# A new order for the attention turn of an attention and soft mixture-of-experts kernel

## The chip, the cores and the metric

The kernel runs on one core of a Trainium2 chip. TensorE (PE) multiplies, VectorE (DVE) reduces and does elementwise work, ScalarE (ACT) copies and takes exponentials, GpSimd (POOL) copies, and SyncE (SP) issues nearly all DMAs. Each engine takes its instructions in program order and waits for others through semaphores. The metric is the device time of one execution in microseconds; the median of three runs is compared.

## What is computed

Block attention over q, k, v of shape (8, 8, 576, 64), in chunks of 64 positions, then a soft mixture of 8 experts over the 4608 rows of 512 numbers that the attention gives.

```
scores = scale * matmul(q_c, k_c^T)             # per (batch, head, chunk): 64 x 64
attn   = exp(scores - max); attn /= sum(attn) + 1e-9
x      = matmul(attn, v_c), heads side by side  # 4608 x 512
logits = x @ phi                                # 4608 x 32
d      = softmax of logits over the rows;    slot_input = d.T @ x
slot_out[e] = relu(slot_input[e] @ w1[e]) @ w2[e]        # 8 experts
c      = softmax of logits over the 32 slots;    out = c @ slot_out
```

All is float32.

## The kernel before

**Stages.** An attention stage of 36 turns, then an expert stage. A turn handles 512 positions of two heads (`unit(t)`: block `n = t // 4`, head pair `t % 4`). Four turns make one block, whose logits and running softmax sums follow in the turns after it. Blocks 0 to 3 come first, then the block made of the last 64 positions of all batches, then 4 to 7.

**One turn t**, by function. SP loads k, q (`load_qk`, 256 KB each) and v (`load_v`, 2 x 128 KB) into three buffers each. POOL reorders k and q by head (`pair_heads`, L166). PE turns each with four transposes (`turn_qk`, L170), ACT copies the turned tiles out of PSUM (`place_qk`, L175 to L191), PE multiplies the scores into `psc` (`scores`, L199), DVE takes the maximum and subtracts it (`s_sub`, L210 and L211), ACT exponentiates (`s_exp`, L217), PE transposes the result into bank 0 of `pav` (`turn_p`, L231), ACT copies it to `at` (`place_p`, L235), PE multiplies with v into all four banks of `pav` (`values`, L244), DVE sums the exponentials and takes reciprocals (`s_sum`, L221 to L224) and normalises `pav` into x (`norm_x`, L252). PE then transposes x (`turn_x`, L260) and ACT copies it to `xT` (`place_x`, L263).

**Once per block**, spread over four successive turns: logits of the block (`logits`, L270) with its running maximum (`maxima`) and exponentials (`weights`); their transposes (`natural`, L310) with `natural_copy` and `shifted` (L322, L324); the partial slot sums (`partial`, L354) and `partial_add` (L365) with `combination`; and `turn_c`, `place_c`.

**What sets the order.** The program text, engine by engine; nothing is reordered. In the loop (L425 to L486) `values` of turn t-1 stands at the end of iteration t and `norm_x` of it at the start of iteration t+1. PSUM has eight banks: `pav` four, `psc` two, `pg` and `ph` one each. Where one of the block steps holds `ph`, the turned q goes to bank 2 of `pav` (`pq = pav[:, 2]`), from iteration 6 on in every iteration.

**Weights.** Of 32 weight tiles of 1 MB (two DMAs of 512 KB each), 17 are loaded during the attention into the pool `wpa` (L426, L427). The next five go to the pool `wpb` (L516), whose memory is that of the attention's buffers, so each waits for the last reader of what lay there; the last ten go to `wpa` tiles as the first expert matmuls (`up`, L532) release them (`refill`). All of these issues stand in SP's one queue. The second expert matmuls are `down` (L566); `combine` and `store` make and write the output.

Of the kernel before, what the change touches and what calls it, by code (L numbers as in the profile page):

```python
# [15 lines left out]
def kernel(  # L16
# [29 lines left out]
    NWB = 5  # L46
    NQ, NV, NX = 3, 3, 7
# [59 lines left out]
    with ExitStack() as actx:  # L107
# [5 lines left out]
        qn = [st.tile([P, 2, 4, D], F32, name=f"qn{i}") for i in range(NQ)]  # L113
        kn = [st.tile([P, 2, 4, D], F32, name=f"kn{i}") for i in range(NQ)]
        vn = [st.tile([P, 2, 2, 2, D], F32, name=f"vn{i}") for i in range(NV)]
        qp = st.tile([P, 4, 2, D], F32, name="qp")
        kp = st.tile([P, 4, 2, D], F32, name="kp")
        qT = [st.tile([P, 8 * CH], F32, name=f"qT{i}") for i in range(2)]
        kT = [st.tile([P, 8 * CH], F32, name=f"kT{i}") for i in range(2)]
        sct = [st.tile([P, 2, 8, 32], F32, name=f"sc{i}") for i in range(2)]  # L120
        at = st.tile([P, 2, 2, P], F32, name="at")
        xr = [st.tile([P, 4, P], F32, name=f"x{i}") for i in range(NX)]
        xT = [st.tile([P, 4, P], F32, name=f"xT{i}") for i in range(NHP)]
# [42 lines left out]
        def pair_heads(t):  # L166
            nc.gpsimd.tensor_copy(kp.rearrange("p j a d -> p a j d"), kn[t % NQ])  # L167
            nc.gpsimd.tensor_copy(qp.rearrange("p j a d -> p a j d"), qn[t % NQ])  # L168
# [6 lines left out]
        def place_qk(t, isk, src):  # L175

            n, b, hp = unit(t)
            o = (kT if isk else qT)[t % 2]
            if isk and b < NB - 1:
                o = o.rearrange("x (c u p j) -> x j u c p", c=8, u=2, j=2)  # L180
                i = src.rearrange("x (j u c p) -> x j u c p", c=8, u=2, j=2)
            elif isk:
                o = o.rearrange("x (c u p j) -> x j u p c", c=8, u=2, j=2)
                i = src.rearrange("x (j u p c) -> x j u p c", c=8, u=2, j=2)
            elif b < NB - 1:
                o = o.rearrange("x (y j) -> x j y", j=4)
                i = src.rearrange("x (j y) -> x j y", j=4)
            else:
                o = o.rearrange("x (c p j) -> x j p c", c=8, j=4)
                i = src.rearrange("x (j p c) -> x j p c", c=8, j=4)  # L190
            nc.scalar.copy(o, i)  # L191
# [58 lines left out]

        def norm_x(t):
            nc.vector.tensor_tensor(  # L252
                xr[t % NX].rearrange("p l (a d) -> p l a d", d=D),
# [4 lines left out]
        def turn_x(t):  # L258
            for l in range(4):
                nc.tensor.transpose(out=pg[:, P * l:P * (l + 1)], in_=xr[t % NX][:, l], identity=ident)  # L260
# [4 lines left out]
        lst, cms, cns = {}, {}, {}  # L265
# [20 lines left out]
        def weights(n):  # L286
            pl = ph[:, 0:P]
            no, nn = nm_run[(n + 1) % 2], nm_run[n % 2]
            eT = sm.tile([P, P], F32, tag="eT", name=f"eT_{n}")
            es = sm.tile([P, 1], F32, tag="es", name=f"es_{n}", bufs=2)  # L290
            nc.scalar.activation(eT, pl, AF.Exp, bias=nn, accum_out=es)
            lT = sm.tile([P, P], F32, tag="lT", name=f"lT_{n}")
# [5 lines left out]
            lst[n] = (eT, lT, al, es)  # L298

        def sums(n):  # L300
            al, es = lst[n][2:]
# [6 lines left out]
        def natural(n):  # L308
            eT, lT = lst[n][:2]
# [3 lines left out]
        def natural_copy(n):  # L313
            eT, lT, al, es = lst[n]
            eN = sm.tile([P, 4, SL], F32, tag="eN", name=f"eN_{n}")
            nc.scalar.copy(eN.rearrange("p l s -> p (l s)"), ph[:, 0:P])
            lst[n] = (eN, lT, al, es)

        def shifted(n):
# [3 lines left out]
            cc = sm.tile([P, 4, SL], F32, tag="cc", name=f"cc_{n}")  # L323
            nc.vector.tensor_tensor(cc, lv, cm.to_broadcast([P, 4, SL]), ALU.subtract)  # L324
            cms[n] = cc

        def combination(n):


            cc = cms.pop(n)  # L330
            nc.scalar.activation(cc, cc, AF.Exp)
# [4 lines left out]
            cn = sm.tile([P, 2, 2, SL], F32, tag="cn", name=f"cn_{n}")  # L336
# [5 lines left out]
            cns[n] = cn  # L342

        def turn_c(n):
            nc.tensor.transpose(out=ph[:, 0:P], in_=cns.pop(n).rearrange("p M w s -> p (M w s)"), identity=ident)
# [4 lines left out]
        def partial(n, dst):  # L350
            eN = lst[n][0]
# [315 lines left out]
```

## Time and profile before

| | us |
|---|---|
| median of three runs (295.39 to 300.87) | 296.06 |
| the profiled execution | 296.35 |
| its span | 294.6 |
| PE busy | 220.6 |
| DVE busy | 146.7 |
| ACT busy | 144.5 |
| POOL busy | 67.0 |

The span is the time from the first to the last instruction of the profiled execution; 1.75 us of its time lie around it. Busy time adds up the instructions of an engine. Matmuls are pipelined, so PE's busy time overstates how much of it is used. The chain of waits names, from the end backwards, what released each instruction that mattered.

### The profile page before, as it was taken

How to read it: one execution, taken by the hardware profiler on the slowest of the kernel's cores; microseconds unless marked ns; L12 is line 12 of the kernel's file. 1: busy time of each engine (PE TensorE's matmuls, PEld its weight loads, DVE VectorE, ACT ScalarE, POOL GpSimd, SP SyncE). 2: the span in 40 equal slices, each digit the busy share in tenths (PEclk: the TensorE clock that was granted, in tenths of full speed). 3: DMA queues.
4: the chain of work that ended last, by engine and by line, in shares of the span. 5: the costliest groups of instructions: out<-in, count | busy, mean ns of one | idle time of the engine just before them, and what ended most of it. 6: DMA issues, size and time to landing. Idle time of an engine off the chain costs nothing.

```text
span 294.6 us, 11946 instructions
## 1 busy us (share of the span) xinstructions
PE 220.6 (75%) x5196; PEld 167.7 (57%) x5196; DVE 146.7 (50%) x339; ACT 144.5 (49%) x277; POOL 67.0 (23%) x149
## 2 busy tenths in 40 slices
PE   8797876877786886886786676796665999978800
PEld 8575765766665675675675665675543235535400
DVE  0386638746656666666756845855521000026800
ACT  1776465655756865764774675565311010025700
POOL 2531133114135852312312411310104000000000
PEclk9999999979999999999999999997955899999955
DMA  7988888667997789797886785642009999997997
GB/s 209 326 277 261 285 249 236 210 207 211 301 262 195 206 267 277 225 301 244 230 286 206 205 255 173 185 122 96 2 2 294 416 396 358 348 296 236 316 328 298
DMA packets 60292, 72.15 MB, mean 245 GB/s; under 512 B 4688, under 2 KB 50768, under 8 KB 60240
## 3 DMA queue, kind: packets, MB, share of 16 engines
q1 hardware_dynamic: 59728, 70.86, 77.0%
q8 instruction: 41, 0.67, 1.0%
q0 software_dynamic: 512, 0.53, 0.7%
q14 instruction: 11, 0.09, 0.1%
HBM read 61.93 MB, written 9.44 MB: 242 GB/s over the span
## 4 chain that ended last, share of the span: by engine, by line
PE 38%; ACT 22%; DVE 20%; issue 6%; DMA 5%; SPq 3%; POOL 1%; DVEq 0%; ACTq 0%; POOLq 0%
ACT qT L191 12%; PE pav L244 7%; PE ph L532 5%; DVE x L252 5%; PE pav L172 5%; PE pav L231 5%; ACT at L235 4%; DVE mx L210 4%; PE ph L270 3%; SPq L102 3%; DMA w<-in_moe_w_dram 3%; DVE sc L211 3%; PE pg L172 3%; DVE su L221 2%; PE ph L132 2%
## 5 line engine op out<-in xcount | busy, mean ns | idle before, releaser
L244 PE MATMUL pav<-vn,at 32*64 32x64 f32 x2304 | 37.9, 232 | 18.4 <-ACT at L235 16.0
L244 PEld LDWEIGHTS pav<-vn,at 32*64 32x64 f32 x2304 | 32.5, 134 | 23.7 <-ACT at L235 20.8
L217 ACT ACTIVATE sc<-sc 128x512 f32<-128x512 f32 x36 | 22.7, 630 | 45.6 <-DVE sc L211 45.6
L167 POOL COPY kp<-kn 128x512 f32<-128x512 f32 x36 | 22.1, 614 | 87.4 <-issue 55.5
L191 ACT COPY qT<-pav 128x512 f32<-128x512 f32 x29 | 31.8, 1097 | 14.8 <-PE pav L231 11.9
L210 DVE TENSOR_REDUCE mx<-psc 128x8 f32<-128x512 f32 x36 | 24.6, 683 | 27.4 <-PE psc L199 27.4
L191 ACT COPY kT<-pg 128x512 f32<-128x512 f32 x36 | 24.3, 675 | 19.0 <-PE pg L172 18.2
L172 PE MATMUL pav<-ident,qp 128*128 128x128 f32 x116 | 18.2, 280 | 19.0 <-DVE x L252 19.0
L199 PE MATMUL psc<-kT,qT 64*64 64x64 f32 x1152 | 26.4, 227 | 2.8 <-issue 2.8
L252 DVE TENSOR_TENSOR x<-pav,rc 128x512 f32<-128x512 f32 x36 | 24.7, 687 | 6.3 <-PE pav L244 6.3
L199 PEld LDWEIGHTS psc<-kT,qT 64*64 64x64 f32 x1152 | 21.0, 136 | 9.4 <-issue 9.4
L172 PEld LDWEIGHTS pav<-ident,qp 128*128 128x128 f32 x116 | 12.9, 143 | 23.2 <-POOL cn L341 9.7
L211 DVE TENSOR_TENSOR sc<-psc,mx 128x512 f32<-128x512 f32 x36 | 24.9, 692 | 1.2
L231 PE MATMUL pav<-ident,sc 128*128 128x128 f32 x144 | 22.3, 278 | 3.8 <-ACT sc L217 3.6
L168 POOL COPY qp<-qn 128x512 f32<-128x512 f32 x36 | 22.1, 614 | 12.6 <-PE pav L172 11.8
L221 DVE TENSOR_REDUCE su<-sc 128x8 f32<-128x512 f32 x36 | 24.4, 678 | 0.9 <-ACT sc L217 0.7
L172 PE MATMUL pg<-ident,kp 128*128 128x128 f32 x144 | 23.2, 284 | 0.9 <-issue 0.5
L235 ACT COPY at<-pav 128x512 f32<-128x512 f32 x36 | 22.8, 633 | 1.9 <-PE pav L231 1.9
L260 PE MATMUL pg<-ident,x 128*128 128x128 f32 x144 | 22.8, 282 | 1.0 <-DVE x L252 0.7
L263 ACT COPY xT<-pg 128x512 f32<-128x512 f32 x36 | 21.6, 600 | 2.4 <-PE pg L260 2.4
L231 PEld LDWEIGHTS pav<-ident,sc 128*128 128x128 f32 x144 | 16.9, 143 | 5.3 <-ACT sc L217 4.8
L172 PEld LDWEIGHTS pg<-ident,kp 128*128 128x128 f32 x144 | 16.3, 143 | 4.4 <-issue 3.2
(86 smaller groups left out, 286.8 us busy)
## 6 DMA issues: line engine op xcount, KB each, us to landing
w<-in_moe_w_dram SPq DMA_DIRECT2D x64, 512.0 KB, 5.9
kn<-in_k_dram SPq DMA_DIRECT2D x32, 256.0 KB, 4.8
qn<-in_q_dram SPq DMA_DIRECT2D x32, 256.0 KB, 5.0
vn<-in_v_dram SPq DMA_DIRECT2D x64, 128.0 KB, 3.7
out_dram<-ob SPq DMA_DIRECT2D x8, 512.0 KB, 4.1
out_dram<-ob SPq DMA_DIRECT2D x4, 1024.0 KB, 7.8
kn<-in_k_dram SPq DMA_DIRECT2D x8, 128.0 KB, 5.4
qn<-in_q_dram SPq DMA_DIRECT2D x8, 128.0 KB, 5.0
```

The lines of the kernel that those rows point to most:

```text
L172: nc.tensor.transpose(out=dst[:, P * j:P * (j + 1)], in_=(kp if isk else qp)[:, j].rearrange("p a d -> p (a d)"), identity=ident)
L191: nc.scalar.copy(o, i)
L199: nc.tensor.matmul(psc[CH * M:CH * (M + 1), a, P * l:P * l + CH], lhsT=qT[t % 2][r, c], rhs=kT[t % 2][r, c], start=True, stop=True,)
L210: nc.vector.reduce_max(mx, pv, axis=AX.X)
L211: nc.vector.tensor_tensor(sct[t % 2].rearrange("p u r i -> p r u i"), pv.rearrange("p r (u i) -> p r u i", u=2), mx.unsqueeze(2).unsqueeze ...
L217: nc.scalar.activation(sct[t % 2], sct[t % 2], AF.Exp, scale=SCALE)
L221: nc.vector.reduce_sum(su, sct[t % 2].rearrange("p u r i -> p r u i"), axis=AX.XY)
L231: nc.tensor.transpose(out=pav[:, 0, o:o + P], in_=sct[t % 2][:, u, 4 * a:4 * (a + 1)].rearrange("p l i -> p (l i)"), identity=ident)
L235: nc.scalar.copy(at.rearrange("p a u x -> p (a u x)"), pav[:, 0])
L244: nc.tensor.matmul(pav[CH * M:CH * (M + 1), l, D * a:D * (a + 1)], lhsT=at[r, a, u, CH * M:CH * (M + 1)], rhs=vv[r, M, a, u, :], start=(u ...
L252: nc.vector.tensor_tensor(xr[t % NX].rearrange("p l (a d) -> p l a d", d=D), pav[:, :, 0:P].rearrange("p l (a d) -> p l a d", d=D), rcs.po ...
L260: nc.tensor.transpose(out=pg[:, P * l:P * (l + 1)], in_=xr[t % NX][:, l], identity=ident)
```

## The change

The loop body is written anew. `scores` and `s_sub` of turn t now stand at the start of iteration t, `values` and `norm_x` of turn t-1 in its middle, and `s_exp`, `turn_p`, `s_sum` and `place_p` of turn t at its end. The turned q always goes to `ph`, and the block steps use `ph` at the end of the iteration. `place_qk` walks its elements in the order of its output instead of that of its input. `partial` makes four matmuls of 512 columns of sixteen with 128, since x now lies in two tiles of four head pairs (`xb`) instead of seven of one. `eT` and `cc`, and `lT` and `cn`, share memory. The loop has one iteration less, and two steps stand behind it. The attention's buffers are laid out in another order, and `wpb` has six tiles instead of five.

```
-    NWB = 5
-    NQ, NV, NX = 3, 3, 7
+    NWB = 6
+    NQ, NV = 3, 3
...
+        qn = tiles("qn", NQ, [P, 2, 4, D])
+        kn = tiles("kn", 1, [P, 2, 4, D])
+        at = st.tile([P, 2, 2, P], F32, name="at")
+        sct = tiles("sca", 1, [P, 2, 8, 32])
+        xT = tiles("xTa", 2, [P, 4, P])
+        vn = tiles("vn", NV, [P, 2, 2, 2, D])
+        sct += tiles("scb", 1, [P, 2, 8, 32])
+        xb = tiles("xb1", 1, [P, 4, DM])
+        qT = tiles("qT", 2, [P, 8 * CH])
+        kT = tiles("kT", 2, [P, 8 * CH])
+        kn += tiles("knb", NQ - 1, [P, 2, 4, D])
...
             if isk and b < NB - 1:
-                o = o.rearrange("x (c u p j) -> x j u c p", c=8, u=2, j=2)
-                i = src.rearrange("x (j u c p) -> x j u c p", c=8, u=2, j=2)
+                o = o.rearrange("x (c u p j) -> x c u p j", c=8, u=2, j=2)
+                i = src.rearrange("x (j u c p) -> x c u p j", c=8, u=2, j=2)
...
             elif b < NB - 1:
-                o = o.rearrange("x (y j) -> x j y", j=4)
-                i = src.rearrange("x (j y) -> x j y", j=4)
+                o = o.rearrange("x (y j) -> x y j", j=4)
+                i = src.rearrange("x (j y) -> x y j", j=4)
...
         def partial(n, dst):
-            eN = lst[n][0]
-            for hp in range(NHP):
-                for l in range(4):
...
+            for l in range(4):
+                nc.tensor.matmul(dst[SL * l:SL * (l + 1), :], lhsT=eN[:, SL * l:SL * (l + 1)],
+                                 rhs=xb[n % 2][:, l], start=True, stop=True)
...
+            if t < NT:
+                scores(t)
+                s_sub(t)
+            if t + 1 < NT:
+                turn_qk(t + 1, 1, pg)
+                place_qk(t + 1, 1, pg)
+            if t + 2 < NT:
+                pair_heads(t + 2, 1)
+            if t >= 1:
+                values(t - 1)
+                norm_x(t - 1)
+            if t + 2 < NT:
+                load_v(t + 2)
+            if t + 1 < NT:
+                turn_qk(t + 1, 0, ph)
+            if t < NT:
+                s_exp(t)
+            if t + 1 < NT:
+                place_qk(t + 1, 0, ph)
+            if t + 2 < NT:
+                pair_heads(t + 2, 0)
+            if t + 5 < NT:
+                load_qk(t + 5)
+            if t >= 2 and bl is None:
+                turn_x(t - 2)
+                place_x(t - 2)
+            if t < NT:
+                turn_p(t)
+                s_sum(t)
+                place_p(t)
             if bl is not None:
                 logits(bl)
+                maxima(bl)
+                turn_x(t - 2)
+                place_x(t - 2)
+                weights(bl)
             if bn is not None:
                 natural(bn)
+                sums(bn)
+                natural_copy(bn)
+                shifted(bn)
+                combination_exp(bn)
             if bp is not None:
                 partial(bp, ph)
+                combination(bp)
+                partial_add(bp, ph)
             if bc is not None:
                 turn_c(bc)
+                place_c(bc)
```

**PE, an iteration in the middle of the loop** (one with `turn_c`). Before:

```order
L345 MATMUL ph<-ident,cn_827 128x128
L172 MATMUL pg<-ident,kp 128x128 x4
L172 MATMUL pav<-ident,qp 128x128 x4
L231 MATMUL pav<-ident,sc_99 128x128 x4
L260 MATMUL pg<-ident,x_102 128x128 x4
L199 MATMUL psc<-kT_98,qT_96 64x64 x16
L244 MATMUL pav<-vn_92,at 64x64 x32
```

The same iteration of the changed kernel, up to the next scores:

```order
L210 MATMUL psc<-kT_100,qT_98 64x64 x16
L183 MATMUL pg<-ident,kp 128x128 x4
L255 MATMUL pav<-vn_94,at 64x64 x32
L183 MATMUL ph<-ident,qp 128x128 x4
L275 MATMUL pg<-ident,xb_96 128x128 x4
L242 MATMUL pav<-ident,scb_95 128x128 x4
L354 MATMUL ph<-ident,lT 128x128
L210 MATMUL psc<-kT_99,qT_97 64x64 x16
```

The scores have moved to the start, q's transposes go to `ph` instead of `pav`, and the transposes of the exponentials (L242) now stand behind `values` of the turn before, one row ahead of the next scores.

**ACT, the same place.** Before:

```order
L217 ACTIVATE sc_100<-sc_100 128x512
L191 COPY kT_98<-pg 128x2x2x8x16
L191 COPY qT_96<-pav 128x4x128
L235 COPY at<-pav 128x512
L263 COPY xT_111<-pg 128x512
```

The changed kernel:

```order
L202 COPY kT_99<-pg 128x512
L228 ACTIVATE scb_95<-scb_95 128x512
L202 COPY qT_97<-ph 128x512
L278 COPY xTb_106<-pg 128x512
L246 COPY at<-pav 128x512
L357 COPY cT<-ph 128x128
```

The exponential stands between the two copies of a turn instead of at its end, `at` is copied last, and the outputs of the k and q copies are one run of 512 elements.

**SP, the first weight tiles in the attention's memory**, with the engines that each waits for (the names DMAHW are slots of the queue). Before:

```order
L102 DMA w_0_1_3869<-in_moe_w_dram 128x1024 [waits DMAHW3_49,Pool_49]
L102 DMA w_0_1_3869<-in_moe_w_dram 128x1024 [waits DMAHW4_49]
L102 DMA w_1_0_3872<-in_moe_w_dram 128x1024 [waits DMAHW5_49,DVE_49,PE_49]
L102 DMA w_1_0_3872<-in_moe_w_dram 128x1024 [waits DMAHW6_49]
L102 DMA w_1_1_3875<-in_moe_w_dram 128x1024 [waits DMAHW7_49]
```

The changed kernel:

```order
L102 DMA w_0_1_3714<-in_moe_w_dram 128x1024 [waits DMAHW3_49,Pool_49]
L102 DMA w_0_1_3714<-in_moe_w_dram 128x1024 [waits DMAHW4_49]
L102 DMA w_1_0_3717<-in_moe_w_dram 128x1024 [waits DMAHW5_49,PE_49]
L102 DMA w_1_0_3717<-in_moe_w_dram 128x1024 [waits DMAHW6_49]
L102 DMA w_1_1_3720<-in_moe_w_dram 128x1024 [waits DMAHW7_49,PE_49,Activation_49]
L102 DMA w_1_1_3720<-in_moe_w_dram 128x1024 [waits DMAHW0_49]
L102 DMA w_2_0_3723<-in_moe_w_dram 128x1024 [waits DMAHW1_49,DVE_49,PE_49]
L102 DMA w_2_0_3723<-in_moe_w_dram 128x1024 [waits DMAHW2_49]
L102 DMA w_2_1_3726<-in_moe_w_dram 128x1024 [waits DMAHW3_49,DVE_49]
L102 DMA w_2_1_3726<-in_moe_w_dram 128x1024 [waits DMAHW4_49]
L102 DMA w_3_0_3729<-in_moe_w_dram 128x1024 [waits DMAHW5_49,PE_49,Activation_49]
```

Before, the second tile (`w_1_0`) waits for DVE's last `norm_x` and for PE's last `partial`, and all tiles behind it in the queue wait with it. In the changed kernel the six tiles wait in turn for: POOL's last q reorder, PE's last q transposes, the last scores, `partial` of block 7, DVE's last sum of a turn, and the last logits.

## Rows read from the trace of the kernel before

**Rows 1.** Windows over stages; first line names columns, times in us, (x) counts instructions.

```profile
core 0: us, PE busy (x) PEld busy (x) DVE busy (x) ACT busy (x) POOL busy (x), PEclk, DMA share, GB/s
20.00:96.60 76.60, 59.74 (x1676) 50.22 (x1671) 48.10 (x107) 46.93 (x87) 23.36 (x48) 0.98 0.84 243
119.23:141.80 22.57, 17.19 (x517) 14.53 (x516) 14.62 (x33) 14.14 (x28) 6.18 (x14) 1.00 0.84 257
204.00:221.00 17.00, 12.34 (x279) 9.01 (x277) 7.51 (x23) 5.01 (x14) 1.33 (x5) 0.70 0.01 2
221.00:265.00 44.00, 38.47 (x437) 17.63 (x439) 4.37 (x20) 5.16 (x12) 3.40 (x13) 0.90 1.01 352
265.00:294.60 29.60, 12.19 (x90) 7.91 (x82) 11.13 (x23) 9.76 (x23) 0.00 (x0) 0.77 0.88 295
```

**Rows 2.** Chain that ended last, one round of four turns: start, us, what.

```profile
119.23 1.08 ACT qT L191
...
121.91 0.70 DVE x L252
...
123.85 1.10 ACT qT L191
...
125.43 1.01 PE pav L244 x55
...
141.80 1.08 ACT qT L191
```

**Rows 3.** Timeline of the same round: start, us, engine, line, operation, out<-in.

```profile
123.21 0.60 PE L231 MATMUL pav<-ident,sc 128*128 128x128 f32 x4
...
123.65 0.60 PE L260 MATMUL pg<-ident,x 128*128 128x128 f32 x4
...
124.18 0.69 PE L199 MATMUL psc<-kT,qT 64*64 64x64 f32 x32
...
125.67 0.69 DVE L211 TENSOR_TENSOR sc<-psc,mx 128x512 f32<-128x512 f32 x1
...
126.37 1.08 PE L270 MATMUL ph<-xT,phi_sb 128*32 128x128 f32 x32
...
126.39 0.63 ACT L217 ACTIVATE sc<-sc 128x512 f32<-128x512 f32 x1 [0.36 <-DVE sc L211]
...
136.34 0.29 DVE L322 TENSOR_REDUCE cm<-ph 128x4 f32<-128x128 f32 x1 [2.49 <-ACT eN L316]
...
137.79 1.08 PE L354 MATMUL ph<-x,eN 128*32 128x128 f32 x32
```

**Rows 4.** Groups by line and form: busy us, mean ns, then idle before them.

```profile
L191 ACT COPY qT<-pav 128x512 f32<-128x512 f32 x29 | 31.8, 1097 | 14.8 <-PE pav L231 11.9 <-DVE su L221 2.8
...
L191 ACT COPY kT<-pg 128x512 f32<-128x512 f32 x36 | 24.3, 675 | 19.0 <-PE pg L172 18.2
...
L235 ACT COPY at<-pav 128x512 f32<-128x512 f32 x36 | 22.8, 633 | 1.9 <-PE pav L231 1.9
...
L374 DVE TENSOR_REDUCE mm<-psc 1x32 f32<-1x128 f32 x1 | 0.3, 279 | 0.5 <-PE psc L371 0.5
```

**Rows 5.** Timeline of the first two turns: the score matmuls.

```profile
10.45 0.69 PE L199 MATMUL psc<-kT,qT 64*64 64x64 f32 x32
...
13.93 0.69 PE L199 MATMUL psc<-kT,qT 64*64 64x64 f32 x32
```

**Rows 6.** Timeline of the end: last score matmuls, first expert matmul.

```profile
204.60 1.14 PE L199 MATMUL psc<-kT,qT 64*64 64x64 f32 x32
...
226.95 5.54 PE L532 MATMUL ph<-w,siT 128*32 128x512 f32 x36
```

**Rows 7.** Waits of the DMA-issuing queue SP: us in total, times, longest.

```profile
SPq L102 <- DVE x L252: 14.5, 1, 14.5
...
SPq L102 <- PE ph L532: 6.4, 1, 6.4
```

**Rows 8.** Chain at the end of the expert stage: the last wait for a weight.

```profile
264.08 0.64 PE po L566 x8
```

More of the change, by code (lines that the diff above doesn't have):

```diff
@@ L112, with tiles @@
         sm = pool("sm", 1)
-        qn = [st.tile([P, 2, 4, D], F32, name=f"qn{i}") for i in range(NQ)]
-        kn = [st.tile([P, 2, 4, D], F32, name=f"kn{i}") for i in range(NQ)]
-        vn = [st.tile([P, 2, 2, 2, D], F32, name=f"vn{i}") for i in range(NV)]
+        def tiles(name, n, shape):
+            return [st.tile(shape, F32, name=f"{name}{i}") for i in range(n)]
+        qn = tiles("qn", NQ, [P, 2, 4, D])
[9 more added lines that the diff above has]
+        kn += tiles("knb", NQ - 1, [P, 2, 4, D])
         qp = st.tile([P, 4, 2, D], F32, name="qp")
         kp = st.tile([P, 4, 2, D], F32, name="kp")
[L118 to L123, printed above, removed]
+        xT += tiles("xTb", 2, [P, 4, P])
+        xb = tiles("xb0", 1, [P, 4, DM]) + xb
+        eT, lT, eN = [sm.tile([P, P], F32, name=x) for x in ("eT", "lT", "eN")]
         pp_ = actx.enter_context(tc.tile_pool(name="pp", bufs=1, space=PSUM))
@@ L313, in natural_copy @@
         def natural_copy(n):
[L314 to L317, printed above, removed]
+            nc.scalar.copy(eN, ph[:, 0:P])
         def shifted(n):
@@ L420 @@
         load_qk(3)
-        pair_heads(1)
+        pair_heads(1, 1)
+        pair_heads(1, 0)
         load_qk(4)
@@ L424 @@
         nc.gpsimd.memset(one, 1.0)
-        for t in range(NT + 2):
+        for t in range(NT + 1):
             want = min(2 * NWA, 2 * NWA * max(t - 1, 0) // (NT - 5))
@@ L430 @@
                               for x in (6, 7, 8, 9)]
-            if t >= 2:
-                norm_x(t - 2)
-            pq = ph
+            if t < NT:
[11 more added lines that the diff above has]
+                load_v(t + 2)
@@ L440 @@
             if bc is not None:
                 turn_c(bc)
-            if (bl, bn, bp, bc) != (None,) * 4:
-                pq = pav[:, 2]
-            if t + 1 < NT:
-                turn_qk(t + 1, 1, pg)
-                turn_qk(t + 1, 0, pq)
-                place_qk(t + 1, 1, pg)
-            if 1 <= t <= NT:
-                turn_p(t - 1)
-            if t + 1 < NT:
-                place_qk(t + 1, 0, pq)
-            if bn is not None:
-                natural_copy(bn)
-            if t >= 2:
-                turn_x(t - 2)
@@ L456 @@
-            if 1 <= t <= NT:
-                place_p(t - 1)
-            if t + 2 < NT:
-                pair_heads(t + 2)
-            if bl is not None:
-                maxima(bl)
-            if bn is not None:
-                shifted(bn)
-            if bp is not None:
-                partial_add(bp, ph)
-            if t < NT:
-                scores(t)
-            if 1 <= t <= NT:
-                s_sum(t - 1)
-                values(t - 1)
-            if t >= 2:
-                place_x(t - 2)
@@ L473 @@
-            if bl is not None:
-                weights(bl)
-                sums(bl)
-            if bc is not None:
-                place_c(bc)
-            if bn is not None:
-                combination(bn)
-            if t + 5 < NT:
-                load_qk(t + 5)
-            if t + 2 < NT:
-                load_v(t + 2)
-            if t < NT:
-                s_sub(t)
-                s_exp(t)
+                place_c(bc)
+        turn_x(NT - 1)
+        place_x(NT - 1)
         n = NB - 1
+        turn_c(n - 1)
@@ L489 @@
+        place_c(n - 1)
         logits(n)
@@ L501 @@
         slots(*ss)
+        combination_exp(n)
         combination(n)
```

52 lines of the change are left out of this document (23 added, 29 removed).

## The prediction

> **What bounds the kernel now.** I read the windows over stages first, then the chain of waits through one round of four turns, then the timeline of that round, and last the end of the program.
>
> In the windows [rows 1] no engine is full during the attention: in the round from 119.23 to 141.80, 22.57 us long, PE is busy 17.2 us, DVE 14.6, ACT 14.1, and the DMA engines 84% of it. So a turn of 22.57 / 4 = 5.64 us is long because of waits between engines, not because of one engine's work. After it come 17 us in which the DMA engines move 2 GB/s, and then 74 us in which they are nearly always busy [rows 1].
>
> The chain [rows 2] shows the loop of waits: the q copy (123.85, 1.10 us), `values` (125.43), `norm_x` (121.91 is that of the turn before), then q's transposes, the exponentials' transposes (123.21 in [rows 3]) and the next q copy. They follow each other because all of them use `pav`: q may be turned into its bank 2 only when `norm_x` has read `pav`, and `values` may write only when q and the exponentials have been copied out. Nothing in that loop overlaps. The reader is to see that 121.91 to 125.43 is one walk around most of it, and that it contains a 1.10 us copy.
>
> In the first turns, where q is turned into `ph`, two score matmuls start 3.48 us apart [rows 5], with the same 1.10 us q copy. This is the nearest row for a turn without that loop.
>
> At the end, SP waits 14.5 us for the last `norm_x` before it may load the second tile into the attention's memory [rows 7], which is the DMA gap of [rows 1]. The last weight is waited for until 264.08 [rows 8], 37.1 us after the first expert matmul at 226.95 [rows 6], and the output follows it.
>
> **The change, part by part.**
>
> *The loop.* With q always in `ph`, `pav` is shared by the exponentials' transposes and `values` alone, and these now have most of a turn between them. I walk one new turn from its scores at 0, on durations of [rows 3]. The subtraction starts 125.67 - 124.18 = 1.49 us later, and the exponential at 126.39 - 124.18 = 2.21 and ends at 2.84. The exponentials' transposes can start at 2.89 and occupy PE for 123.65 - 123.21 = 0.44, so the next scores can start at 3.33. Two other conditions end close to it. `values` starts after the scores (0.55 of issue) and k's transposes (0.44), at 1.0, and ends at 2.0 (duration 1.01, [rows 2]); `norm_x` takes 0.70 after a 0.1 us handover and another 0.13 passes before PE, so the transposes wait until 2.94. The q copy follows the exponential on ACT and ends near 3.40. So a turn without block work takes about 3.45 us. PE's own rows fill nearly all of it: four sets of transposes of 0.44, scores 0.55, `values` 126.37 - 125.43 = 0.94 together make 3.25.
>
> Block work comes on top. Between the exponentials' transposes and the next scores PE gets the logits (1.0), the partial sums (about 0.9 in place of 1.0, the same columns in fewer instructions; from 1.08 each in [rows 3]) and three single transposes (0.35), 2.3 us in a round. DVE's two steps on the transposed logits (0.29 each, [rows 3]) now wait for a copy that stands behind `at` on ACT, and stand ahead of the next maximum on DVE: about 0.8 late there, and 0.3 behind `partial_add`. Waits for `ph` until the q copy is done add some 0.5. That is 3.95, and a round is 4 x 3.45 + 3.95 = 17.75 us, or 4.44 a turn.
>
> *The q and k copies.* q goes from a store in steps of 16 bytes to a contiguous store with a strided PSUM read. Contiguous on both sides costs 633 ns (L235), the old q copy 1097, the old k copy 675 [rows 4]. No ACT row reads PSUM in steps, so the cost lies between 633 and 1097 for each. The nearest row is DVE's reduction that reads 128 PSUM elements in steps of 128 bytes: 279 ns [rows 4], against 290 for one of 128 contiguous elements (L322, [rows 3]). A stepped read costs nothing there, so I take 633, and it stands in the walk above.
>
> [...]
>
> *What is late next: the loads.* A turn loads 0.786 MB of q, k and v, and 34 weight pieces of 0.524 MB come over 31 turns: 1.36 MB a turn. At their busy share the DMA engines give 257 / 0.84 = 306 GB/s in one window and 243 / 0.84 = 289 in another [rows 1]; I take 300. That is 1.36 / 0.300 = 4.55 us a turn, more than the 4.44 of the engines. k and q are loaded for five turns ahead and v for two, so a late load is absorbed for a while, but not a lasting deficit. I take 4.55.
>
> Scores of turn 35 then start at 10.45 + 35 x 4.55 = 169.7 us instead of 204.60 [rows 5, 6]. This is the main term, 34.9 us.
>
> *From the last scores to the experts.* Now 226.95 - 204.60 = 22.35 us [rows 6]. The chain of the last block is the same; ahead of its logits the new text has `turn_x`, the c transposes and POOL's reorder for block 7, which I put at 0.7 us more by the same walk. First expert matmul: 169.7 + 23.05 = 192.75.
>
> *The weight tiles.* The six tiles wait one after another for readers that finish during turns 33 to 36 or with the last logits, so all twelve pieces are in long before the first expert matmul: the 14.5 us wait [rows 7] goes. The gap doesn't vanish, it moves: the other 18 pieces still need `wpa` tiles that the first experts release, some 5 us after their start (SP waits for L532 now too, [rows 7]). 18 x 0.524 = 9.44 MB at 352 GB/s [rows 1] take 26.8, so the last weight is there 31.8 us after the first expert matmul instead of 37.1. The output follows: its first stores wait for PE's `down`, not for weights, but they no longer share the DMA engines with the last weights and the second half can be made earlier. I take 5 us of the 5.3: from the first expert matmul to the end 294.6 - 226.95 - 5 = 62.65.
>
> *Others.* The memory shared by `eT` and `cc`, and `lT` and `cn`, adds waits on POOL's work of the block before, two turns old by then: nothing. POOL keeps its two copies a turn.
>
> Sum: 192.75 + 62.65 = 255.4 us of span, and 1.75 around it as in the profiled execution (296.35 against 294.6): **257 us**. The median of the runs, 296.06, is 0.3 below that execution; I don't correct for it.
>
> **The rivals.**
>
> *Stepped PSUM reads are slow (0.15).* Both copies take 1.10 us. The q copy then ends near 3.87 in the walk and each turn grows by 0.46: 17.75 + 1.84 = 19.6 a round, 4.9 a turn. 10.45 + 171.5 + 23.05 + 62.65 + 1.75 = 269 us. Against it speaks L374 [rows 4]; for it, that this row is DVE's.
>
> *The loads fall behind (0.10).* At 289 GB/s and with loads that arrive late now and then, a turn takes 5.0: 273 us. For it: the DMA engines are at 84% already [rows 1]. Against: the loads stand two to five turns ahead.
>
> *The change does not free the loop (0.06).* Some wait I don't see replaces that on `pav`, and a turn takes 5.3: 283 us. Against it speaks the 3.48 us of the first turns [rows 5].
>
> *Slower (0.04).* A stepped PSUM read costs far more than the dearest copy shown. If each copy takes p, the q copy adds p - 0.63 to a turn, and the k copy, which stands ahead of the exponential, adds p - 1.0 from 1.0 on. The round reaches 22.57 us plus the half microsecond that the end gives back at p = 1.48; at 1.6 it is 24.0, and the time 308 us. The dearest 512-element copy in the trace takes 1097 ns [rows 4].
>
> *Better than forecast (0.05).* The engines' 4.44 holds, the six turns before the first block step run at 3.48, and the loads keep up: 10.45 + 20.9 + 29 x 4.44 = 160.1 us to the last scores, and 247.5 in all.
>
> **How the numbers follow.** 0.60 is left for the forecast, 250 to 264 us by itself. The range of 248 to 272 takes in the first rival and part of the second; some 0.2 lies outside, mostly above. Below 290 us the change counts as faster by over 2%, about what a measurement of this kernel tells from no change. All but the slower rival and half of the third lie there: faster 0.93, same 0.03, slower 0.04.
>
> **What would show it.** Right: scores of successive turns 4.3 to 4.8 us apart; the q and k copies at 0.60 to 0.68; a DMA share near 1 in the attention; weight DMAs in the last turns; the first expert matmul at 185 to 200 us. Wrong: copies near 1.1 or above; SP or POOL waiting for loads with PE idle behind them; `norm_x` still ahead of q's transposes in the chain; the DMA gap before the experts as long as now.

## The result and the profile after

The changed kernel takes **283.19 us** (median of 280.54 to 284.83), the kernel before 296.15 in the same comparison: a ratio of 0.954, 95% interval 0.943 to 0.965. It is faster, by 13 us and not by the 39 that were predicted. The profiled execution took 284.39 us, 282.6 of it span. One of the kernel's four runs (284.83) fell into a slow state; the median of the other three, 281.98, is what the experiments below are compared with.

The stages of the changed kernel, as windows with the columns of [rows 1]: two rounds of four turns, the last scores up to the first expert matmul in two pieces, the experts, the output.

```profile
101.94:122.47 20.53, 18.20 (x493) 14.09 (x492) 14.66 (x34) 12.38 (x29) 7.72 (x16) 1.00 0.93 290
122.47:144.19 21.72, 18.59 (x493) 14.19 (x492) 14.47 (x34) 12.55 (x29) 6.23 (x13) 1.00 0.88 288
193.58:210.00 16.42, 11.19 (x233) 6.47 (x232) 7.27 (x22) 6.17 (x19) 1.33 (x5) 0.90 0.73 249
210.00:216.80 6.80, 2.90 (x11) 2.46 (x11) 2.09 (x8) 0.47 (x2) 1.72 (x7) 0.50 0.29 120
216.80:252.80 36.00, 35.19 (x423) 15.25 (x422) 3.09 (x13) 4.68 (x10) 1.69 (x7) 0.95 0.83 272
252.80:282.60 29.80, 13.57 (x90) 9.37 (x90) 11.31 (x23) 9.73 (x23) 0.00 (x0) 0.76 0.93 308
```

These two rounds take 20.5 and 21.7 us where [rows 1] had 22.57 and the prediction 18.2 (four turns of 4.55); over turns 4 to 35 a round takes 21.8 in the mean, (193.58 - 24.32) / 31 x 4. PE is busy for 18.2 to 18.6 us of a round shown; before it was 17.19. The pages' shares of the chain that ended last, before and after, say the same: PE has become the bound.

```profile
PE 38%; ACT 22%; DVE 20%; issue 6%; DMA 5%; SPq 3%; POOL 1%; DVEq 0%; ACTq 0%; POOLq 0%
PE 72%; issue 10%; DVE 7%; ACT 5%; POOL 1%; DVEq 0%; POOLq 0%; ACTq 0%
```

PE's timeline from the second of those rounds, in the notation of [rows 3]:

```profile
122.47 0.33 PE L210 MATMUL psc<-kT,qT 64*64 64x64 f32 x5
123.33 0.68 PE L210 MATMUL psc<-kT,qT 64*64 64x64 f32 x27 [0.54 <-issue]
123.94 0.66 PE L183 MATMUL pg<-ident,kp 128*128 128x128 f32 x4
124.53 1.01 PE L255 MATMUL pav<-vn,at 32*64 32x64 f32 x64
125.47 0.66 PE L183 MATMUL ph<-ident,qp 128*128 128x128 f32 x4
126.49 0.63 PE L242 MATMUL pav<-ident,sca 128*128 128x128 f32 x4 [0.36 <-DVE xb L267]
127.05 0.64 PE L285 MATMUL ph<-xTa,phi_sb 128*32 128x128 f32 x16
127.51 0.40 PE L285 MATMUL ph<-xTb,phi_sb 128*32 128x128 f32 x7
129.10 0.52 PE L285 MATMUL ph<-xTb,phi_sb 128*32 128x128 f32 x9 [1.20 <-issue]
...
133.95 0.27 PE L322 MATMUL ph<-ident,eT 128*128 128x128 f32 x1
135.12 0.27 PE L323 MATMUL ph<-ident,lT 128*128 128x128 f32 x1 [0.90 <-issue]
```

Little of the old loop is left: the one wait for `norm_x` (`xb` L267) is 0.36 us here, and all such waits in the attention add up to 3.0 us in 8 places, where the kernel before had 19.0 in 20. But PE halts three times in the midst of a group of like matmuls whose inputs are all there: after 5 of 32 score matmuls, after 23 of 32 of the logits, between two transposes. The releaser is "issue", which is nothing that the profile shows. Count the matmul records between two halts: from 123.33 to the halt ahead of 129.10 there are 27 + 4 + 64 + 4 + 4 + 16 + 7 = 126, and each has a weight load beside it. From 129.10 to the halt ahead of 135.12 it is 126 again. The page's row of the queue named "instruction" fits one packet to each such block: PE's 4980 matmuls and as many weight loads are 255 to a packet.

```profile
q8 instruction: 39, 0.64, 0.9%
```

0.64 MB in 39 packets is 16 KB a packet. Over the attention (9.65 to 193.58 us) PE's halts put down to "issue" add up to 19.4 us in 19 places; between the scores of turns 0 and 35 in the kernel before it was 5.3 us in 6. The two largest groups after, as line, releaser, us in total, times, longest:

```profile
PE pav L255 <- issue: 8.9, 7, 2.9
PE psc L210 <- issue: 6.0, 6, 1.7
```

One more wait belongs to them: 1.16 us at 117.63, put down to ACT's copy of `at`, fall 125 records behind the halt that ends at 110.74.

### The profile page after: what moved, and what is told of

It reads as the page before. It is cut to its first block, busy times and chain, and to the rows that moved or that the text cites. A ratio compares the mean times of both kernels' runs of the same rounds, so it can differ in the third digit from the quotient of the medians.

```text
span 282.6 us, 11578 instructions
## 1 busy us (share of the span) xinstructions
PE 228.0 (81%) x4980; PEld 164.1 (58%) x4980; DVE 147.5 (52%) x339; ACT 129.2 (46%) x277; POOL 67.5 (24%) x149
## 4 chain that ended last, share of the span: by engine, by line
PE 72%; issue 10%; DVE 7%; ACT 5%; POOL 1%; DVEq 0%; POOLq 0%; ACTq 0%
PE pav L255 12%; PE psc L210 7%; PE pg L183 7%; PE pav L242 7%; PE ph L536 6%; PE ph L183 5%; PE pg L275 5%; PE po L570 5%; PE pf L597 4%; PE ph L285 4%; PE ph L361 2%; PE ph L143 2%; DVE xb L267 2%; ACT xTa L278 2%; DVE mx L221 1%
## 5 line engine op out<-in xcount | busy, mean ns | idle before, releaser
L267 DVE TENSOR_TENSOR xb<-pav,rc 128x512 f32<-128x512 f32 x36 | 24.8, 690 | 16.2 <-PE pav L255 15.3
L210 PEld LDWEIGHTS psc<-kT,qT 64*64 64x64 f32 x1152 | 21.5, 134 | 19.8 <-issue 17.7
L202 ACT COPY qT<-ph 128x512 f32<-128x512 f32 x36 | 21.0, 583 | 13.5 <-PE ph L183 13.1
L179 POOL COPY kp<-knb 128x512 f32<-128x512 f32 x24 | 14.7, 611 | 49.3 <-PE pg L183 32.5
L183 PE MATMUL ph<-ident,qp 128*128 128x128 f32 x144 | 24.7, 295 | 0.7 <-issue 0.7
L275 PE MATMUL pg<-ident,xb 128*128 128x128 f32 x144 | 23.2, 284 | 0.1
L275 PEld LDWEIGHTS pg<-ident,xb 128*128 128x128 f32 x144 | 17.0, 145 | 3.1 <-issue 2.2
L183 PEld LDWEIGHTS ph<-ident,qp 128*128 128x128 f32 x144 | 15.8, 145 | 3.4 <-POOL kp L179 0.6
L242 PE MATMUL pav<-ident,sca 128*128 128x128 f32 x72 | 12.4, 296 | 5.7 <-DVE xb L267 2.6
L603 DVE COPY ob<-pf 128x256 f32<-128x256 f32 (+1 forms) x26 | 12.5, 522 | 8.0 <-PE pf L597 7.8
L536 PE MATMUL ph<-w,siT 128*32 128x512 f32 x128 | 16.2, 657 | 0.0
L597 PE MATMUL pf<-so,cT 32*128 32x256 f32 (+1 forms) x104 | 14.4, 561 | 0.5 <-ACT so L586 0.5
```

The costliest lines, as they stand in the source:

```text
L179: nc.gpsimd.tensor_copy(dst.rearrange("p j a d -> p a j d"), src)
L183: nc.tensor.transpose(out=dst[:, P * j:P * (j + 1)], in_=(kp if isk else qp)[:, j].rearrange("p a d -> p (a d)"), identity=ident)
L210: nc.tensor.matmul(psc[CH * M:CH * (M + 1), a, P * l:P * l + CH], lhsT=qT[t % 2][r, c], rhs=kT[t % 2][r, c], start=True, stop=True,)
L242: nc.tensor.transpose(out=pav[:, 0, o:o + P], in_=sct[t % 2][:, u, 4 * a:4 * (a + 1)].rearrange("p l i -> p (l i)"), identity=ident)
L267: nc.vector.tensor_tensor(x_of(t).rearrange("p l (a d) -> p l a d", d=D), pav[:, :, 0:P].rearrange("p l (a d) -> p l a d", d=D), rcs.pop(t ...
L275: nc.tensor.transpose(out=pg[:, P * l:P * (l + 1)], in_=x_of(t)[:, l], identity=ident)
```

## The experiments

**Theories.** *Supply*: PE is fed by blocks of some 250 instructions, and halts where a block is used up before the next is there. Rivals: PE's own work, the copies, the loads, or waits that moved. Diffs are abridged, with several loops on one line.

**1. Fewer instructions, same columns.**

```diff
-for l, M, a: matmul(psc[64M:, a, 128l:128l+64], lhsT=qT[r, c], rhs=kT[r, c])          # 16, 64 columns
+for M, a:    matmul(psc[64M:, a, four l], lhsT=qT[r, 256M:256M+64], rhs=kT[r, 256M:256M+256])  # 4
-for a, M, u, l: matmul(pav[64M:, l, 64a:64a+64], lhsT=at[r, a, u, M], rhs=vv[r, M, a, u])  # 32
+for M, l:       matmul(pav[64M:, l, 0:256], lhsT=at[r, 0, 0, M], rhs=vv[r, M])             # 8
```

> The changed kernel with the matmuls of scores and values made four times as wide and a quarter as many (4 instead of 16 calls for scores, 8 instead of 32 for values): the same number of columns go through PE on the same row and column groups, with 24 instead of 96 matmul records a turn. It computes other numbers there (one query chunk's weights for four key chunks), so only its time counts. Supply theory: in the trace after the change PE halts about four times a round for 0.9 to 1.5 us, waiting for nothing the profile shows, and between two halts there are always 126 matmul and 126 weight-load records; the instruction queue moves 39 packets of 16 KB. So PE is fed by the count of its instructions. A round falls from about 517 records to about 230, its halts from four to two or fewer; a round from 21.1 us (mean of 20.5 and 21.7) to 17.5 to 19, scores of turn 35 from 193.6 to 160 to 170, the time from 283 to 250 to 262. Rival, PE's own work and its handovers set the turn: same columns, same time, 278 to 286. Rival, the loads set the turn (0.9 of the DMA engines): no change either, and SP's loads are then waited for.

(The 517 records named there are those of a round before; a round of the changed kernel has 493.) Measured: **250.22 us**, ratio to before 0.851 (0.841 to 0.860). The scores of one turn and of that four later in its timeline:

```profile
102.04 0.66 PE L209 MATMUL psc<-kT,qT 64*64 64x256 f32 x8
119.78 0.66 PE L209 MATMUL psc<-kT,qT 64*64 64x256 f32 x8
```

Its page's row of the instruction queue:

```profile
q8 instruction: 19, 0.31, 0.5%
```

A round settles at 17.74 us (18.48 at most), and PE has no wait for "issue" in the attention. It also waits for no load at this pace: the DMA engines move 336 GB/s at a share of 1.05 in 97 to 142 us, against the 300 that the prediction allowed. But the wide `values` takes 0.62 instead of 0.94 us, so part of the gain is PE's work.

**2. The same with PE's work put back.** Three transposes of a constant into a free part of the bank stand behind `values` in each turn.

```diff
+for _ in range(3): transpose(out=pav[:, 3, 384:512], in_=ident)
```

> The first experiment's wide matmuls, with three extra transposes behind values in each turn (0.11 us each) that make up for the 0.33 us that the wide values takes less: PE's work a turn is that of the changed kernel, and only the count of its instructions differs (27 instead of 96 records for these parts). Supply theory: the saving of the first experiment was the halts, so at most 0.33 us a turn comes back, less where PE waited for others: 252 to 262. If it came from PE's shorter work: 275 to 284.

Measured: **260.34 us**, ratio 0.884 (0.878 to 0.890). Scores of one turn, of that four later, and of turn 35:

```profile
103.91 0.66 PE L209 MATMUL psc<-kT,qT 64*64 64x256 f32 x8
122.58 0.66 PE L209 MATMUL psc<-kT,qT 64*64 64x256 f32 x8
169.32 0.66 PE L209 MATMUL psc<-kT,qT 64*64 64x256 f32 x8
```

A round is 18.67 us, and turn 35 starts at 169.3; the prediction had 169.7, the changed kernel 193.58. With equal PE work (`values`, the three transposes and those of q take 1.44 us together, as `values` and those of q do in the changed kernel) and less than half of the attention's matmul records, 281.98 - 260.34 = 21.6 us go, and PE's waits for "issue" with them. Between the two profiled executions it is 25.0. So the halts for instructions cost some 22 us, and PE's shorter work accounts for the other 10 of the first experiment. There are fewer weight loads too; that they are not what saved the time is shown by experiment 4, where all of them are left.

**3 and 4. A block by itself, with idle and with full DMA engines.** Both put 1024 independent calls of the shape of `values` (2048 records) ahead of the first transposes; the second also issues the 34 weight pieces at the start.

```diff
+for _ in range(32): for M, m, l: matmul(pav[64M:, l, ...], lhsT=ident[r, 64M:64M+64], rhs=ident[r, 0:64])
```

> The changed kernel with 1024 more matmul calls (2048 records) of the shape of those of values, ahead of the first transposes; they depend on nothing and their results are overwritten. From about 16 us on the DMA engines have nothing left to move. At the 0.94 us that 64 such records take in a turn they would take 30 us if nothing else held PE. Theory A, the halts come because the instruction packets queue behind the loads: 30 to 36 us for the stretch, no halts of a microsecond. Theory B, each block of 126 records has a delay of its own (a packet started about 3 us after the block before it and PE went on 2.3 to 2.8 us behind the packet's start): 16 blocks of 3.5 to 5.5 us each, 56 to 88 us. The rest of the kernel is as before, so the time is 283 plus the stretch.

> The same 1024 calls with all 34 weight pieces of the first pool (17.8 MB) issued at the start, so that the DMA engines are full during the stretch (17.8 MB at 0.3 to 0.35 MB/us is 51 to 59 us). Theory A (packets queue behind the loads): the blocks of 126 records take 4 to 6 us here and 2 us with idle DMA engines. Theory B (a delay of their own): the blocks take the same in both. A further reading is the attention behind it, which now has no weight pieces to load, 0.79 instead of 1.36 MB a turn: by A its halts nearly go and a round takes 17.5 to 18.5 us; by B a round stays at 20 to 21.5.

Measured: 342.16 and 339.74 us, one execution each. The timeline of the idle case:

```profile
20.73 1.76 PE L425 MATMUL pav<-ident 32*64 32x64 f32 x128 [1.97 <-issue]
...
34.82 2.68 PE L425 MATMUL pav<-ident 32*64 32x64 f32 x128 [0.78 <-issue]
```

Its windows row over the four blocks from 20.73 on, columns as in [rows 1]:

```profile
20.73:34.82 14.09, 9.02 (x513) 8.38 (x513) 0.00 (x0) 0.00 (x0) 0.00 (x0) 0.68 0.02 5
```

The timeline of the loaded case:

```profile
21.39 2.68 PE L426 MATMUL pav<-ident 32*64 32x64 f32 x128 [3.79 <-issue]
27.59 2.68 PE L426 MATMUL pav<-ident 32*64 32x64 f32 x128 [3.52 <-issue]
```

Its windows row over four blocks:

```profile
21.39:46.18 24.79, 10.72 (x513) 10.04 (x513) 0.00 (x0) 0.00 (x0) 0.00 (x0) 0.50 1.02 406
```

With idle DMA engines (share 0.02) a block of 128 records takes 14.09 / 4 = 3.5 us, with full ones (1.02) 24.79 / 4 = 6.2. Its own work is 1.76 us in the first idle block shown and 2.68 in the other, the same as in the loaded ones, where the granted clock is 0.50 (over the four idle blocks it is 0.68 in the mean); both are shorter than the cycle, so the clock doesn't set it. The loaded trace shows this by itself: its loads are over by 57.5 us, and with the same 2.68 us of work the blocks then come 3.7 us apart.

```profile
61.47 2.68 PE L426 MATMUL pav<-ident 32*64 32x64 f32 x128 [1.05 <-issue]
65.20 2.68 PE L426 MATMUL pav<-ident 32*64 32x64 f32 x128 [1.05 <-issue]
```

Both theories hold a part: the cycle has a length of its own, and full DMA engines add 2.7 us to it. Narrow windows of the DMA view place the packets: in both cases PE goes on 2.2 to 2.9 us behind the start of a packet, but the packet starts 1.0 to 1.6 us after PE went on with the block before in the idle case and 3.6 to 3.7 us after it in the four loaded blocks. What the loads add is a delay ahead of the packet. In the changed kernel the packets for the halts that end at 129.10 and 135.12 start at 126.51 and 132.58: 3.2 and 3.5 us after PE went on, near the loaded case, and 2.6 and 2.5 us before it goes on again.

The loaded kernel's attention has no weights left to load (DMA share 0.60 from 100 to 230 us). Its halts for "issue" add up to 5.0 us in 8 places, against 19.4 in 19, and a round takes 19.1 us in the mean, (250.54 - 121.55) / 27 x 4, against 21.8. In the last three rounds no halt is left. Scores of one turn there and of that four later:

```profile
214.00 0.69 PE L210 MATMUL psc<-kT,qT 64*64 64x64 f32 x32
232.27 0.69 PE L210 MATMUL psc<-kT,qT 64*64 64x64 f32 x32
```

18.27 us a round, with all instructions of the changed kernel. So the halts need both: about four blocks a round, used at the pace of PE's work, and DMA engines so busy that a block takes longer to come than to use. The mean lies below the second theory's 20 to 21.5 for the attention and above the first one's 17.5 to 18.5, which only the last rounds meet; the first one's stand for the idle stretch (no halts) is refuted.

**5. The old copies in the new order.** `place_qk` as before.

> The changed kernel with the old copies of q and k (read in order, store in steps): 1.10 and 0.68 us instead of 0.58. By the walk of the prediction the q copy lies in the turn's path: 0.5 us a turn, 18 us, 301. By the trace after, where PE is busy or waits for instructions for nearly the whole round, the longer copy partly fills a halt: 283 to 292.

Measured: 285.25 us, ratio 0.967 (0.959 to 0.976); the interval meets that of the changed kernel. The q copy takes 1092 ns again, but 18 us don't come back; at most a few do. The largest of PE's waits for the copy and for "issue", as line, releaser, us in total, times, longest:

```profile
PE psc L210 <- ACT qT L202: 2.4, 6, 1.2
PE pav L255 <- issue: 6.7, 5, 2.9
```

Over the attention PE waits 8.5 us for the q copy, against 0.7 in the changed kernel, but its halts for "issue" fall from 19.4 to 11.2 us: the one wait takes the place of the other. So in the changed kernel the copies' order is worth little; what it is worth where nothing halts was not measured.

**6. The new copies alone in the kernel before.**

> The kernel before with one part of the change alone, the copies of q and k that write in order: 0.58 us each instead of 1.10 and 0.68, as the trace after shows them. In the kernel before the q copy lies in the loop over the bank of four, so by the prediction's reading of that loop each turn becomes up to 0.5 us shorter: 35 turns give 18 us, 278. If the halts for instructions also fill the loop of the kernel before (they last 0.6 to 2 us in its trace where nothing else is waited for), part of it is lost to them: 282 to 292. That the loop does not bound the kernel before: 294 to 296.

Measured: 288.34 us, ratio 0.977 (0.968 to 0.986): 7 us instead of up to 18. PE's waits there:

```profile
PE pav L172 <- DVE x L252: 16.8, 20, 1.6
...
PE pav L244 <- issue: 3.9, 4, 2.0
```

The loop through `norm_x` is still waited for, and PE's halts for "issue" over the attention are 11.9 us in 12 places instead of 5.3 in 6: a shorter loop shows more of them.

**7. The wide matmuls alone in the kernel before.**

> The kernel before with the same wide matmuls as in the first experiment (a quarter as many in scores and values, same columns, other numbers computed). If the loop of waits over the bank of four bounds it, and halts for instructions mostly lie in time in which PE would wait anyway, it gains little: some 0.3 us a turn because the 16 wide matmuls of values take 0.61 instead of 0.94 us, and some of the halts, 275 to 288. If the halts alone made the kernel before slow, it falls as far as the changed kernel did (33 us): 260 to 266. Then the new order of a turn would be worth little by itself.

Measured: 288.65 us, ratio 0.980 (0.972 to 0.987). The loop bounds the kernel before, as its waits show:

```profile
PE pav L172 <- DVE x L250: 23.7, 21, 1.6
PE pav L242 <- ACT at L235: 16.1, 29, 0.7
```

Fewer and shorter instructions alone give 6.8 us (295.46 - 288.65), the change alone 13, both together 45. Each hides behind the other.

**8 and 9. Fewer instructions with the whole reference computed.** `v` is kept with zeros beside it, so that one matmul of `values` covers two chunks; the ninth also gives the exponentials' transposes a bank of their own.

```diff
-vn = tiles("vn", NV, [P, 2, 2, 2, D])
+vn = tiles("vn", NV, [P, 2, 2, 2, 2, D])       # zeros for the other chunk of the pair; NWA = 16
-for M in range(2): dma(vv[:, M], src[M])
+for M, l: dma(vv[32l:32l+32, M, :, l % 2], src[l, M])
-for a, M, u, l: matmul(..., lhsT=at[32 rows], rhs=vv[32 rows, M, a, u])
+for a, M, u, h: matmul(..., lhsT=at[64 rows], rhs=vv[64 rows, M, a, :, u])
```

> A version of the changed kernel that computes the whole reference with fewer instructions: v is kept with zeros beside it, so that one matmul of values serves two neighbouring chunks (64 rows, 128 columns) instead of one (32 rows, 64 columns): 16 calls a turn instead of 32, 80 matmul records a turn instead of 112. It costs columns: values goes from 0.94 us to about 1.2 (twice as many columns, on half as many row groups at once). The larger v tiles take the memory of one weight tile, so 16 instead of 17 are loaded during the attention, and v comes in eight pieces a turn instead of two. Supply theory: a round has about 128 records fewer, one halt of about 1 us fewer and shorter ones left, PE has 1 us more work; a round from 21.1 to 19 to 20, the time 266 to 276. If PE's own work bounds the turn: 283 to 292.

> As the version before, with the exponentials' transposes moved to a bank of their own (values now needs two banks of the four, so one is free): they no longer wait for norm_x, and values no longer waits for the copy of the exponentials. The trace after shows such waits as 3.4 us in all. Supply theory: 262 to 276, at most 4 us below the version before. If PE's work bounds it: no difference between the two.

Measured: **345.4** and **341.5 us**, ratios 1.168 (1.156 to 1.180) and 1.157 (1.146 to 1.167). Both expectations failed. In the eighth, from the page, the shares of the chain and the costliest group:

```profile
DMA 46%; PE 27%; SPq 14%; issue 3%; DVE 3%; POOL 2%; ACT 1%; POOLq 0%; DVEq 0%; ACTq 0%
L256 PE MATMUL pav<-vn,at 64*64 64x128 f32 x1152 | 80.5, 309 | 37.1 <-DMA vn<-in_v_dram 33.5
```

The longest wait of its DMA-issuing queue, as in [rows 7]:

```profile
SPq L171 <- DMA w<-in_moe_w_dram: 49.5, 27, 2.9
```

The eight small transfers of `v` a turn are held up: SP waits 49.5 us until weight transfers have landed before it issues the next piece of `v`, the DMA engines are busy for only 0.64 of 100 to 200 us, and PE waits 33.5 us for `v`. `values` also takes 1.62 us undisturbed, more than the 1.2 expected. This says nothing on the supply theory: another bound came in. Why SP waits there stays open. The orders of SP name eight slots that its transfers take in turn (DMAHW0 to DMAHW7); whether eight small ones a turn use these up is not shown.

**10 and 11. Fewer records by bf16.** First q and k alone, then the exponentials and `v` too. Only the precision of these operands is lower.

```diff
-qT, kT = tiles(..., F32)
+qT, kT = tiles(..., BF16)                      # the copies of ACT round
-at = st.tile([P, 2, 2, P], F32); vv = vn[t % 3]
+at = st.tile([P, 2, 2, P], BF16); vv = vb[t % 2]   # eleven: POOL rounds v into vb, one copy a turn
```

> The changed kernel with q and k rounded to bf16 by the copies that place them (ACT writes them as bf16, the same 36 + 36 copies). In the trace after a call of scores makes two matmul records in fp32; in bf16 it should make one: 96 instead of 112 matmul records a turn, and PE's 0.63 us for the scores falls towards half. Precision is lower there, nothing is left out. Supply theory: 64 records fewer a round, half a halt fewer, and 1.2 us less PE work: a round from 21.1 to 19 to 20, the time 266 to 274. If only PE's time counts: 1.2 us a round, 272 to 274. If neither: 283.

> As the one before, with the exponentials (rounded by their copy on ACT) and v (rounded by one more copy a turn on POOL, about 0.6 us) in bf16 too, so that values makes 32 instead of 64 records: 64 matmul records a turn instead of 112, all else fp32. Supply theory: about 325 records a round instead of 517, 2.6 blocks of 126 instead of 4.1, with 6.6 us of PE time for each, so the halts go (a block took 6.2 us at the slowest, with the DMA engines full); a round of 16.5 to 18.5, then bound by the loads and the handovers; the time 246 to 258. If PE's time alone counts (0.3 of scores and 0.4 of values a turn, 2.9 us a round): 257 to 262. If POOL's extra copy gets in the way: above 262.

Measured: **274.54 us**, ratio 0.934 (0.927 to 0.941), half a microsecond above both theories' ranges, so it doesn't tell them apart; and **251.42 us**, ratio 0.851 (0.843 to 0.859), inside its range and below the 257 that PE's time alone would give. The eleventh is the fastest version of these that computes the whole reference, at bf16 operands in the attention's products. Its PE waits:

```profile
PE pav L251 <- ACT sca L237: 8.8, 14, 1.2
PE pav L264 <- POOL vb L188: 5.0, 5, 1.8
```

PE's halts for "issue" add up to 0.6 us in its attention (16.6 us in the tenth); now PE waits for the softmax and for POOL's copies of v, which in turn wait 9.4 us for the loads of v (DMA share 1.03 from 97 to 142 us).

**12. Five weight tiles instead of six** in the memory that the attention leaves.

```diff
-NWB = 6
+NWB = 5
```

> The changed kernel with five instead of six weight tiles in the attention's memory, its buffers laid out as in the change. The trace after shows PE busy without a wait for weights from 216.88 to 254.68: the experts' own work on PE takes 36.0 us up to the last half of the second product, not the 31.8 us of loading that the prediction took as the bound. By that reading the sixth tile gives little: from the first expert matmul to the end 65.8 to 68 us with five tiles (65.8 with six, 67.65 before). By the prediction's reading the loads are the bound, and a missing tile (two pieces of 0.52 MB at 352 GB/s) costs 3 us: 68.8 or more.

From the first expert matmul (215.75) to the end 283.7 - 215.75 = 67.95 us of one execution. PE waits for a weight twice more, briefly:

```profile
251.23 0.64 PE L570 MATMUL po<-w,hz 128*32 128x256 f32 x8 [0.20 <-DMA w<-in_moe_w_dram]
252.67 0.64 PE L570 MATMUL po<-w,hz 128*32 128x256 f32 x8 [0.80 <-DMA w<-in_moe_w_dram]
```

A missing tile costs 2.2 us against the 65.8 of six tiles, not the 3 of its loading time; 1.0 of it are the two waits shown, and where the rest goes is open in a single execution.

## Why the prediction was right and wrong

| step | predicted | changed kernel |
|---|---|---|
| q and k copies | 633 ns | 583 ns |
| turn without block work | 3.45 us | 3.73 us, 20.60 - 16.87 |
| round of four turns | 18.2 us | 21.8 us in the mean |
| scores of turn 35 | 169.7 us | 193.58 us |
| from there to the first expert matmul | 23.05 us | 23.23 us |
| from there to the end | 62.65 us | 65.8 us |
| around the span | 1.75 us | 1.79 us |

The misses are 23.9, 0.2 and 3.1 us, which is the 27.2 by which the profiled execution lies above the sum.

**The loop: right.** It bounded the kernel before (experiment 7), and the new order frees it: `norm_x` makes PE wait 0.36 us in the round shown, and q's transposes follow `values` at once. Alone it shows little of its worth: the whole change gives 13 us, and 45 together with fewer instructions (experiments 1 and 7).

**The copies: right in size, wrong in worth.** Rows of after against [rows 4]:

```profile
L202 ACT COPY kT<-pg 128x512 f32<-128x512 f32 x36 | 21.0, 583 | 35.8 <-PE pg L183 35.2
L202 ACT COPY qT<-ph 128x512 f32<-128x512 f32 x36 | 21.0, 583 | 13.5 <-PE ph L183 13.1
```

The stepped PSUM read cost ACT nothing: 583 ns, against 589 for the contiguous copy of the exponentials in the same trace. The rival of slow reads falls. The copies' worth in the new order is small (experiment 5).

**The turn: the step that failed.** "So a turn without block work takes about 3.45 us" and the round of 17.75 made from it priced PE as so many instructions of so many nanoseconds, and put what it takes to bring the instructions to it at nothing. So did the 4.55 us of the sum, the larger of that walk and the loads. A turn took 5.25 us, 183.9 / 35, and the halts are what made turn 35 come 23.9 us late: without them, with the same PE work, it starts at 169.3 us and not at 193.58 (experiment 2).

The walk itself is near, and a little short. Without halts a round takes 18.27 us with all instructions (experiment 4) and 18.67 with the same PE work (experiment 2), against 17.75. The two turns after the first show where:

```profile
16.87 0.69 PE L210 MATMUL psc<-kT,qT 64*64 64x64 f32 x32
20.60 0.69 PE L210 MATMUL psc<-kT,qT 64*64 64x64 f32 x32
```

The 3.73 us between them are PE's work alone, which the prediction added up to 3.25: its sets of four transposes take 0.50 to 0.59 us back to back, not 0.44, and the scores 0.62, not 0.55. (The walk's parts of the block work add up to 3.9, not 3.95.) Two close agreements are luck. The 17.74 us of experiment 1 have a `values` that is 0.3 us shorter a turn than the walk's. And turn 35 at 169.3 us in experiment 2, where 169.7 was predicted, is made of early turns of 3.85 us and later ones of 4.67, not of turns of 4.55.

The loads, which the prediction took as the bound of a turn (4.55 us at 300 GB/s), reach 336 GB/s where PE asks for it (experiment 1); they act through the instructions that they delay (a block after 6.2 instead of 3.5 us, experiments 3 and 4).

Signs of it were there in the page of the kernel before, in the group of the scores' weight loads and in the instruction queue:

```profile
L199 PEld LDWEIGHTS psc<-kT,qT 64*64 64x64 f32 x1152 | 21.0, 136 | 9.4 <-issue 9.4
q8 instruction: 41, 0.67, 1.0%
```

The 9.4 us of "issue" looked small. Part of the halts may have fallen into time in which PE waited for `norm_x` or ACT anyway: a shorter loop shows more of them (experiment 6). How many did is not shown. The second row is 0.67 MB in 41 packets, 16 KB each, and PE's 5196 matmuls and as many weight loads there are 253 to a packet; what a packet costs PE, neither row tells. The prediction didn't use them.

**The third rival** gave 283 us for "Some wait I don't see", with 5.3 us a turn, and the time is there. But it put the wait in place of the one on `pav`, and there it is not: the right number is luck.

**The last scores to the experts: right**, 23.23 against 23.05.

**The weight tiles: mechanism right, size wrong.** The gap moved as foretold: SP no longer waits 14.5 us for `norm_x` [rows 7] but for the first experts:

```profile
SPq L102 <- PE ph L536: 15.3, 2, 15.0
```

But "the last weight is there 31.8 us after the first expert matmul" took the loads as the bound of that stage. PE's own work is longer. In the chain it goes from the first expert matmuls to the output without a wait for a weight:

```profile
216.88 8.82 PE ph L536 x64
...
252.78 1.06 PE pf L597 x12
```

That is 36.0 us from 216.81, which [rows 6, 8] put at 264.72 - 226.95 = 37.8 before, where PE waits 1.7 us for weights in three places. The gain is 1.8 us, not 5; the output behind it takes 29.8 us as before. Experiment 12 agrees.

**The range** missed because its cases all took PE's instructions as given; the rival of the loads had the right resource and the wrong way in which it acts.

## What to carry to other kernels

Before a change that packs an engine's work closer, count the instructions that it issues and how fast: many small matmuls can use up instructions faster than they arrive (here a block of 256 came after 3.5 to 6.2 us), and the time shows only as unexplained halts inside a group, at equal counts of records (126 here). Fewer, wider matmuls, or a type that needs fewer records (16 instead of 32 for the scores of a turn in bf16, experiment 10), then pay twice: of the 32 us of experiment 1 the halts were some 22 and PE's work 10. A wait that is removed while such halts are there gains little, since a halt takes its place (7.8 us less of the one, 8.2 more of the other between experiment 5 and the changed kernel). And of a stage with both loads and work, price both before the slower one is named.

## What the runs showed of the hardware

- PE went through its program in blocks of 256 instructions (513 matmuls and 513 weight loads over four blocks, experiments 3 and 4), 16 KB each (0.64 MB in 39 packets, changed kernel). With idle DMA engines a block that was used up at once was followed by the next after 3.5 us (experiment 3) to 4.0 (experiment 4, behind its loads), with full ones (406 GB/s) after 6.2 (experiment 4).
- The delay under load lay ahead of the packet (3.6 to 3.7 instead of 1.0 to 1.6 us), not behind its start (2.2 to 2.9 us in both; experiments 3 and 4).
- ACT read PSUM in steps and wrote SBUF in order in 583 ns for 128 x 512 fp32 (changed kernel); the other way round the q copy took 1092 to 1097 ns and the k copy 675 to 677 (experiment 5 and kernel before).
- Splitting `v` from two into eight transfers a turn left the DMA engines at a share of 0.64 and made SP wait 49.5 us for transfers issued earlier (experiment 8).
